# A two-layer MLP after sliding-window attention: its second product by Strassen's seven products

## The chip, the core and the metric

The kernel runs on one core of one Trainium2 chip. The engines are called as in the profile: PE is TensorE (matrix products), PEld its weight loads, DVE is VectorE, ACT is ScalarE, POOL is GpSimd, SP is SyncE, which here only issues DMAs. SBUF is the on-chip working memory, with 128 partitions; PSUM is the accumulator memory that PE writes to, in banks of 512 fp32 per partition. A semaphore is what one engine waits on for another. The metric is the device time of one launch in microseconds (us), as the median of several runs. Lower is better.

## The reference

Attention with a window of 128 and a bias that falls with distance, then layer norm, a two-layer MLP with ReLU, and the residual. Nothing else is computed.

```
# q, k, v: [8 batches, 8 heads, 576 positions, 64], fp32
scores = q k^T / 8 - slope[h] * |i - j|;  kept where 0 <= i - j < 128
attn   = softmax(scores);  x = (attn v), heads side by side   # x: [8, 576, 512]
mu  = mean(x);  var = mean((x - mu)**2)                       # over the 512 columns
xn  = (x - mu) / sqrt(var + 1e-06) * g_ln                     # g_ln: [512]
out = x + max(xn @ w_ch1, 0) @ w_ch2                          # w_ch1 [512, 2048], w_ch2 [2048, 512]
```

## The kernel before, in words

**Tiling.** The 8 x 576 rows are 36 blocks of 128 rows. `attention(i)` (line 571) takes one block from loads to the transposed and centred rows that the MLP reads. `mlp(c)` (line 932) takes one chunk of blocks; `CHUNKS` (line 267) has chunks of 3, 3, 2 and then seven of 4 blocks. "From the fourth chunk on" means these last seven, 28 blocks.

**The order.** Every piece of work is a `Task` with an engine, an assumed duration, the tasks that it needs, and a due value `v`. `Plan.run` (line 118) plays the whole kernel through as a list schedule: whenever an engine is free, it gives it the task that is ready and has the lowest `v`. The instructions are then emitted in that order, so each engine's queue is fixed before the launch. For a PE task that needs another engine's result, `SLACK` (line 294) makes the planner assume that the result comes 1.0 us later than it thinks. Attention is given a `v` that is 1.6 chunks ahead of the MLP (`av`, line 365; `LEAD`, `SPAN`). `PICK`, `PRI` and `HOLD` are tables of hand-set engine choices and shifts of `v`; their entries for MLP tasks are for the first three chunks.

**Attention of a block.** Scores on PE into `sc` (line 750), exponentials on ACT (line 798), a mask product on DVE (line 805), the product with v on PE into a bank of `fb` (line 822), then on DVE the reciprocal of the softmax sum (line 839) and the normalised rows `xb` (line 843, which also sums them through an accumulator that is read out as an instruction of its own). DVE then forms the mean (line 876), `xs` = (x - mean) * g (line 883, with g spread over the partitions in `g_t`, fp32), and the statistics (lines 864 and 870). A transposing DMA on SP's queue puts `xs` into `xt` (line 912). `rstd` = exp(-0.5 ln(var + eps)) is made on ACT, once for a chunk (lines 923 and 926). It isn't needed by the first product: since ReLU commutes with a positive factor of each row, it is applied at the very end.

**The MLP of a chunk.** First product: 16 groups A of four matmuls, each over up to 512 rows of the chunk (line 944), with 128 x 128 of `w1sb` as the stationary operand; ReLU on ACT or DVE puts each group into `ht` (lines 954 and 956). Second product: for each block 16 matmuls (B, line 972) with 128 x 128 of `ht` as the stationary operand and 512 columns of `w2sb` streamed; then one DVE instruction makes rstd * product + x (line 980) and one DMA on SP's queue stores the block (line 988). The last block is cut at column 384, so that most of its result is away before the last matmuls are done.

**Memory.** PE's work for the MLP, the transposes and the product with v share four PSUM banks, `fb`. `ht` has two buffers, `xt` three, `xb` sixteen blocks, `ot` (the results) four blocks. `qs`, `ks`, `qs16` and `ks16` are only used for the loads of blocks 0 to 5. POOL issues most loads of q, k, v and of the weights; SP the transposing DMAs and the stores. `keep_warm` (line 1009) fills PE with dummy products in the first 24 us.

Of the kernel before, what the change touches and what calls it, by code (L numbers as in the profile page):

```python
# [241 lines left out]
def kernel(  # L242
# [54 lines left out]
    HOLD = {'Za0': 3.13, 'k10.i': 55.05, 'cT0.11': 9.73, 'mreg20': 36.97, 'k8.i': 46.36, 'dist2a': 4.68}  # L297
    HEADS = 3
# [44 lines left out]
    xb = ring("xb", 16, [P, d_model], FP16)  # L343
# [3 lines left out]
    ot = ring("ot", 4, [P, d_model], FP32)  # L347
    st = ring("st", 4, [P, nc.vector.BN_STATS_DIM], FP32)
    mv = ring("mv", 4, [P, CB, nc.vector.BN_AGGR_DIM], FP32)
    lv = ring("lv", 2, [P, CB], FP32)  # L350
# [4 lines left out]
    g_row, one_t = ot[3][0:1, :], ot[2][0:1, 0:P]  # L355
# [93 lines left out]
    d_g = add("Gc", {"ACT": 0.6, "DVE": 0.69}, e_gc, [t_g], av(0, 4.5), rel="G")  # L449

# [120 lines left out]
    def attention(i):  # L571
# [240 lines left out]
        nm = []  # L812
        for half in range(2):
# [27 lines left out]
            def e_nm(e, b, half=half, key=key):  # L841
                pp = fb[plan.held[key][1]][:, 0 : 4 * (D + 1)].rearrange("p (h d) -> p h d", d=D + 1)
                nc.vector.scalar_tensor_tensor(  # L843
                    out=xb[i][:, 256 * half : 256 * half + 256].rearrange("p (h d) -> p h d", d=D),
# [5 lines left out]
                    accum_out=sums[i][:, half : half + 1],  # L850
# [4 lines left out]
            sums.writes(i, n_)  # L855
            rec.reads(2 * i + half, n_)
            xb.writes(i, n_)
            nm.append(n_)

        c = CHUNK_OF[i]  # L860
        j = i - FIRST[c]

        def e_bn(e, b):
            nc.vector.bn_stats(out=st[i][:, :], in_=xb[i][:, :])  # L864
        stats_v = max(av(i, 6.5), FIRST[c] / CB * SPAN - STATS_LEAD)
# [9 lines left out]
        def e_mu(e, b):  # L875
            nc.vector.tensor_scalar(
                out=mean[i][:, :], in0=sums[i][:, 0:1], scalar1=sums[i][:, 1:2], scalar2=1.0 / d_model, op0=ALU.add, op1=ALU.mult,
            )
        mu = add(f"mu{i}", ("DVE", 0.21), e_mu, nm, av(i, 6.5))
        sums.reads(i, mu); mean.writes(i, mu)  # L880

        def e_xs(e, b):
            nc.vector.scalar_tensor_tensor(  # L883
                out=xs[i][:, :], in0=xb[i][:, :], scalar=mean[i][:, 0:1], in1=g_t[:, :],
                op0=ALU.subtract, op1=ALU.mult,
            )
        xs_ = add(f"xs{i}", ("DVE", 0.75), e_xs, [mu, d_g], av(i, 6.6))
        mean.reads(i, xs_)
        xs.writes(i, xs_)
        xs_done[i] = xs_  # L890
        bn.deps.append(xs_)

        if i < X_BY_DMA:
# [15 lines left out]
            xt.writes(c, xt_)  # L909
        else:  # L910
            def e_xd(e, b):
                nc.sync.dma_start_transpose(out=xt[c][:, :, j * P : j * P + P], in_=xs[i][:, :])
            xi, xt_ = plan.transfer(f"XT{i}", "SP", 1.2, 0.85, 0.5, e_xd, [xs_], av(i, 7.0))
            xs.reads(i, xt_)
            xt.writes(c, xi)
        xt_done[i] = xt_

        if j == CHUNKS[c] - 1:
# [12 lines left out]

    def mlp(c):
# [4 lines left out]
        relu = []  # L937
        for f in range(NFB):
            key = f"A{c}.{f}"
            vm = v0 + f * per  # L940
# [7 lines left out]
            a = add(key, ("PE", 0.216 * nb), e_a, done + [t_w[f // 4][1]], vm, acq=("fb", key))  # L948
            xt.reads(c, a)

# [8 lines left out]
            relu.append(r_)  # L959
        for j in range(nb):  # L960
            i = FIRST[c] + j
            cuts = (0, 3 * P, d_model) if i == NBLK - 1 else (0, d_model)
            for c0, c1 in zip(cuts, cuts[1:]):
                key = f"B{i}" if c1 - c0 == d_model else f"B{i}.c{c0}"
                last = None
                for f0 in range(0, NFB, 4):
# [9 lines left out]
                    last = add(f"{key}.{f0}", ("PE", 0.864 * (c1 - c0) / d_model), e_b, relu[f0 : f0 + 4] + [t_w[4 + f0 // 4][1], last], vm, acq=("fb", key))  # L976
                    ht.reads(c, last)

                def e_o(e, b, i=i, j=j, key=key, c0=c0, c1=c1):
                    nc.vector.scalar_tensor_tensor(  # L980
                        out=ot[i][:, c0:c1], in0=fb[plan.held[key][1]][:, 0 : c1 - c0], scalar=rstd[c][:, j : j + 1],
                        in1=xb[i][:, c0:c1], op0=ALU.mult, op1=ALU.add,
                    )
# [20 lines left out]
    for c in range(len(CHUNKS)):  # L1004
        mlp(c)
# [46 lines left out]
```

## Time and profile before

| what | value |
| --- | --- |
| median of three runs (lowest, highest) | 320.42 us (320.11, 321.05) |
| span of the profiled execution | 317.5 us |
| mean granted TensorE clock over the span | 1.000 |
| PE busy | 311.3 us (98%) |
| DVE busy | 189.5 us (60%) |
| ACT busy | 161.0 us (51%) |
| POOL busy | 100.6 us (32%) |
| first product on PE (line 944) | 134.5 us busy, 640 matmuls |
| second product on PE (line 972) | 134.6 us busy, 592 matmuls |

The span runs from the first to the last instruction of one execution; the time of a run also holds what lies around it, 2.9 us between this span and the median. A matmul is pipelined, so the duration of one in the trace is longer than the distance from it to the next; how fast PE goes is read from the starts of long streaks. "Busy" counts overlapping matmuls once.

### The profile page before, as it was taken

The numbers are of one execution on the slowest core, as the hardware profiler recorded it, in microseconds if no ns is written. First come the engines' busy times: TensorE is split into PE (matmuls) and PEld (weight loads), VectorE is DVE, ScalarE is ACT, GpSimd is POOL, SyncE is SP. The second block draws the span as 40 slices with busy tenths as digits, with TensorE's granted clock in tenths as the row PEclk, the third lists the DMA queues.
The fourth block names the chain that finished last, engine by engine and source line by source line (L and its number), as shares of the span: only waits on it lengthen the run. The fifth ranks groups of instructions, "written<-read, shape, count | busy, mean of one in ns | idle before, by whom it ended". The sixth has DMA issues, their size and how long they took to land.

```text
span 317.5 us, 6575 instructions
## 1 busy us (share of the span) xinstructions
PE 311.3 (98%) x2580; PEld 178.3 (56%) x2580; DVE 189.5 (60%) x523; ACT 161.0 (51%) x258; POOL 100.6 (32%) x133
## 2 busy tenths in 40 slices
PE   8999999999999999999999999999999999999995
PEld 7777656765955544555555555545555455445543
DVE  3496788889866646764676467648654676221012
ACT  3657816872836732674267426742574257305600
POOL 5663469765633355434263234000000000000000
PEclk9999999999999999999999999999999999999999
DMA  8999999999999999999999999834600240011011
GB/s 176 248 219 205 196 140 167 168 148 117 162 178 158 174 138 173 171 166 131 171 189 154 100 135 172 108 52 116 118 17 19 83 85 18 21 66 66 2 66 66
DMA packets 156049, 40.15 MB, mean 126 GB/s; under 512 B 142577, under 2 KB 151025, under 8 KB 156018
## 3 DMA queue, kind: packets, MB, share of 16 engines
q0 software_dynamic: 101680, 16.65, 75.7%
q1 hardware_dynamic: 54336, 23.08, 40.9%
q8 instruction: 20, 0.33, 0.5%
q14 instruction: 11, 0.09, 0.1%
q10 hardware_dynamic: 2, 0.00, 0.0%
HBM read 36.70 MB, written 9.44 MB: 145 GB/s over the span
## 4 chain that ended last, share of the span: by engine, by line
PE 91%; DMA 5%; DVE 1%; SPq 0%; POOL 0%; issue 0%
PE fb L944 40%; PE fb L972 39%; PE sc L750 6%; PE fb L822 5%; DMA vxp<-in_v_dram 3%; DMA qs<-in_q_dram 2%; PE fb L714 1%; PE fb L1011 0%; SPq L483 0%; PE fb L897 0%; PE sc L766 0%; PE fb L666 0%; POOL qs L648 0%; POOL w1sb L562 0%; DVE mmix L469 0%
## 5 line engine op out<-in xcount | busy, mean ns | idle before, releaser
L972 PE MATMUL fb<-w2sb,ht 128*128 128x512 f16 (+2 forms) x592 | 134.6, 373 | 0.1
L944 PE MATMUL fb<-xt,w1sb 128*128 128x512 f16 (+2 forms) x640 | 134.5, 359 | 0.0
L956 ACT ACTIVATE ht<-fb 128x512 f16<-128x512 f32 (+2 forms) x142 | 79.5, 560 | 52.4 <-PE fb L944 50.7
L798 ACT ACTIVATE probs<-sc 128x1024 f16<-128x1024 f32 (+1 forms) x72 | 67.8, 973 | 69.2 <-PE sc L750 69.0
L944 PEld LDWEIGHTS <-w1sb 128*128 128x128 f16 x640 | 68.9, 114 | 47.1
L972 PEld LDWEIGHTS <-ht 128*128 128x128 f16 x592 | 54.0, 98 | 57.4 <-issue 0.3
L980 DVE SCALAR_TENSOR_TENSOR ot<-fb,rstd,xb 128x512 f32<-128x512 f32 (+2 forms) x37 | 27.2, 736 | 42.1 <-PE fb L972 41.8
L499 POOL DMA_DIRECT2D vx<-in_v_dram x36 | 30.4, 849 | 38.0 <-PE fb L822 21.1
L499 POOL DMA_DIRECT2D qk<-in_q_dram x34 | 28.5, 839 | 42.7 <-DMA qkt<-qk 22.6
L805 DVE TENSOR_TENSOR probs<-probs,mreg 128x1024 f16<-128x1024 f16 (+1 forms) x46 | 30.3, 676 | 13.9 <-ACT probs L798 13.7
L839 DVE RECIPROCAL rec<-fb 128x4 f32<-128x4 f32 x72 | 12.7, 179 | 36.7 <-PE fb L822 36.4
L822 PEld LDWEIGHTS <-probs 128*128 128x128 f16 x544 | 24.9, 97 | 13.1 <-issue 0.6
L843 DVE SCALAR_TENSOR_TENSOR xb<-fb,rec 128x256 f16<-128x256 f32 x72 | 30.3, 422 | 1.9
L499 POOL DMA_DIRECT2D qk<-in_k_dram x34 | 28.7, 847 | 7.0 <-DMA qk<-in_k_dram 2.1
L883 DVE SCALAR_TENSOR_TENSOR xs<-xb,mean,g_t 128x512 f16<-128x512 f16 x36 | 26.9, 748 | 0.7
L822 PE MATMUL fb<-vx,probs 128*128 128x65 f16 x496 | 27.2, 193 | 0.1
L864 DVE BATCH_NORM_STATS2 st<-xb 128x6 f32<-128x512 f16 x36 | 24.6, 683 | 0.0
L750 PEld LDWEIGHTS <-qkt 64*128 64x128 f16 x496 | 14.9, 94 | 11.9 <-issue 10.1
L750 PE MATMUL sc<-qkt 64*128 64x128 f16 x264 | 18.0, 216 | 0.0
L750 PE MATMUL sc<-qkt,qkt 64*128 64x128 f16 x208 | 14.7, 219 | 0.0
L954 DVE TENSOR_SCALAR ht<-fb 128x384 f16<-128x384 f32 (+2 forms) x18 | 10.4, 579 | 6.3 <-PE fb L944 6.0
L1011 PE MATMUL fb<-warm_t 128*128 128x128 f16 x122 | 10.6, 251 | 1.1 <-DVE warm_t L400 1.1
(71 smaller groups left out, 128.6 us busy)
## 6 DMA issues: line engine op xcount, KB each, us to landing
out_dram<-ot SPq DMA_DIRECT2D x35, 256.0 KB, 4.0
vx<-in_v_dram POOLq DMA_DIRECT2D x28, 128.0 KB, 9.8
qk<-in_q_dram POOLq DMA_DIRECT2D x26, 128.0 KB, 9.2
qk<-in_k_dram POOLq DMA_DIRECT2D x26, 128.0 KB, 10.1
w1sb<-in_moe_w_ch_dram POOLq DMA_DIRECT2D x4, 512.0 KB, 11.1
w2sb<-in_moe_w_ch_dram POOLq DMA_DIRECT2D x4, 512.0 KB, 14.2
ks<-in_k_dram SPq DMA_DIRECT2D x4, 256.0 KB, 6.5
qs<-in_q_dram SPq DMA_DIRECT2D x4, 256.0 KB, 6.2
```

The costliest lines, as they stand in the source:

```text
L499: nc.gpsimd.dma_start(out=dst(p0, n), in_=src[b, :, s0 : s0 + n, :].rearrange("h p d -> p h d"))
L750: nc.tensor.matmul(scs[half][:, g, c0 : c0 + P], kt[rows, 1, hp, :], qkt[i][rows, 0, hp, :], start=not bias, stop=True, skip_group_check=True,
L798: nc.scalar.activation(out=o, in_=n_, func=AF.Exp, scale=inv_sqrt_d)
L805: en.tensor_tensor(out=pv, in0=pv, in1=mask[:, 2 * half : 2 * half + 2, :, lo:], op=ALU.mult)
L822: nc.tensor.matmul(pp[:, hh * (D + 1) : hh * (D + 1) + D + 1], probs[i][:, bank, slot, side * P : side * P + P], vx[i if side else before] ...
L843: nc.vector.scalar_tensor_tensor(out=xb[i][:, 256 * half : 256 * half + 256].rearrange("p (h d) -> p h d", d=D), in0=pp[:, :, 0:D], scalar ...
L864: nc.vector.bn_stats(out=st[i][:, :], in_=xb[i][:, :])
L883: nc.vector.scalar_tensor_tensor(out=xs[i][:, :], in0=xb[i][:, :], scalar=mean[i][:, 0:1], in1=g_t[:, :], op0=ALU.subtract, op1=ALU.mult,)
L944: nc.tensor.matmul(fb[b][:, 0:n_], w1f[f // CB][:, kb, f % CB, :], xt[c][:, kb, 0:n_], start=(kb == 0), stop=(kb == NKB - 1),)
L956: nc.scalar.activation(out=ht[c][:, f, 0:n_], in_=src, func=AF.Relu)
L972: nc.tensor.matmul(pm[:, 0 : c1 - c0], ht[c][:, f, j * P : j * P + P], w2sb[f // CB][:, f % CB, c0:c1], start=(f == 0), stop=(f == NFB - 1),)
L980: nc.vector.scalar_tensor_tensor(out=ot[i][:, c0:c1], in0=fb[plan.held[key][1]][:, 0 : c1 - c0], scalar=rstd[c][:, j : j + 1], in1=xb[i][: ...
```

## The change

The second product of a chunk is, with H the 512 x 2048 rows after ReLU and W the 2048 x 512 matrix `w_ch2`, cut in two halves each way. Instead of eight products of halves it computes seven, of sums and differences of the halves (the form of Strassen's method with fewest additions, due to Winograd). Each of the seven is 16 matmuls that stream 256 columns; before, a chunk's second product was 64 matmuls that stream 512.

- `weight_sums` forms four sums of the quarters of `w_ch2` once, eight DVE subtractions, in the memory of `qs` and `ks`.
- In each of the seven chunks DVE forms four sums of quarters of `ht`, in two instructions each (`sa`, `sb` into the memory of `qs16` and `ks16`; `sc`, `sd` in place in `ht`).
- The products alternate between two PSUM banks, X and Y. DVE adds what lies in a bank to the result (`ra` to `rg`, seven instructions of 512 elements; before, four). A product that accumulates onto the one before it in its bank, or starts the bank anew, waits for the read of that bank.
- The residual and the products can only be added if no factor of a row comes after. So in these chunks the rows are normalised ahead of the first product: `xs` = (x - mean) * rstd, with mean and rstd per partition, and g is multiplied into the rows of `w_ch1` on chip (`scale_weights`, 16 DVE instructions, after the third chunk's first product has read `w_ch1`). rstd is now formed for two blocks at a time and stands ahead of `xs`; the two blocks' transposing DMAs come after it. The mean of line 876 and the accumulator of line 843 fall away in these chunks.
- `gcol` is g with its 512 values down the partitions, from four small matmuls.
- The groups A of these chunks run in the order 0, 8, 1, 9, ..., so that the halves' sums can start early.
- `xb` is kept and released by chunk and `ot` by two blocks (three buffers of two); the cut of the very last block at column 384 is gone; in the last chunk each block is stored in two halves of its columns.

```diff
+    SEVEN = 3
+    SUMS_V = 40.0
...
-    xb = ring("xb", 16, [P, d_model], FP16)
+    xb = ring("xb", 4, [P, CB, d_model], FP16)
-    ot = ring("ot", 4, [P, d_model], FP32)
+    ot = ring("ot", 3, [P, 2, d_model], FP32)
+    gcol = sb("gcol", [P, NKB], FP32)
...
+    def e_gk(e, b):
+        for kb in range(NKB):
+            nc.tensor.matmul(fb[b][:, kb : kb + 1], g_row[:, kb * P : kb * P + P], one_t[:, 0:1], start=True, stop=True)
...
+    t_gk = add("Gk", ("PE", 0.5), e_gk, [t_g], av(2, 4.0), acq=("fb", "Gk"))
+    d_gk = add("Gkc", ("DVE", 0.2), e_gkc, [t_gk], av(2, 4.5), rel="Gk")
...
+        fast = c >= SEVEN
...
-                    accum_out=sums[i][:, half : half + 1],
+                    accum_out=None if fast else sums[i][:, half : half + 1],
...
+        elif j % 2 == 0:
+            todo = []
+        else:
+            def e_ln(e, b):
+                nc.scalar.activation(out=lv[i][:, 0:2], in_=mv[c][:, j - 1 : j + 1, 1], func=AF.Ln, bias=eps_t[:, :])
+            def e_rs(e, b):
+                nc.scalar.activation(out=rstd[c][:, j - 1 : j + 1], in_=lv[i][:, 0:2], func=AF.Exp, scale=-0.5)
...
+            for x, y in ((i - 1, j - 1), (i, j)):
+                def e_xs(e, b, x=x, y=y):
+                    nc.vector.tensor_scalar(
+                        out=xs[x][:, :], in0=xb[c][:, y, :], scalar1=mv[c][:, y, 0:1], scalar2=rstd[c][:, y : y + 1],
+                        op0=ALU.subtract, op1=ALU.mult,
+                    )
+                xs_ = add(f"xs{x}", ("DVE", 0.3), e_xs, [rs], av(x, 6.6))
...
+    def weight_sums():
...
+            for n, (dst, a, b_) in enumerate(((o[0], b12, b11), (o[2], b22, b12), (o[1], b22, o[0]), (o[3], b21, o[1]))):
+                def emit(e, b, dst=dst, a=a, b_=b_):
+                    nc.vector.tensor_tensor(out=dst, in0=a, in1=b_, op=ALU.subtract)
+                t = add(f"sumT{h}.{n}", ("DVE", 0.69), emit, got[h][-1:] + [t_w[4 + h][1], t_w[6 + h][1]], SUMS_V)
...
+    def scale_weights():
+        for m in range(CB):
+            def emit(e, b, m=m):
+                for kb in range(NKB):
+                    nc.vector.tensor_scalar(out=w1sb[m][:, kb, :], in0=w1sb[m][:, kb, :], scalar1=gcol[:, kb : kb + 1], scalar2=None, op0=ALU.mult)
+            scaled.append(add(f"scaleW{m}", ("DVE", 0.9), emit, plain[m] + [d_gk, t_w[m][1]], FIRST[SEVEN] / CB * SPAN - 8.0))
+
+    def seven(c, relu, v0):
+        A, B_ = slice(0, FOURTH), slice(FOURTH, 2 * FOURTH)
...
+        def product(n, k, key, lhs, rhs, first, deps):
+            for p in range(2):
+                for h in range(2):
+                    def emit(e, b, p=p, h=h):
+                        o = fb[plan.held[key][1]][:, FOURTH * p : FOURTH * p + FOURTH]
+                        for f in range(CB * h, CB * h + CB):
+                            nc.tensor.matmul(o, lhs(f, p), rhs(f), start=first and f == p == 0, stop=f == F2 - 1, skip_group_check=True)
+                    t = add(f"{k}{c}.{p}{h}", ("PE", 0.436), emit, deps[h] + [last.get((key, p))], v0 + (4 * n + 2 * p + h) * step, acq=("fb", key))
...
+        def read(name, key, out, in1, deps, n, rel=None):
+            def emit(e, b):
+                src = fb[plan.held[key][1]][:, :].rearrange("p (n c) -> p n c", n=2)
+                nc.vector.tensor_tensor(out=out, in0=src, in1=in1, op=ALU.add)
+            return add(f"{name}{c}", ("DVE", 0.75), emit, deps, v0 + (4 * n + 4) * step - 12.0, rel=rel)
...
+            s1.append(sums("sa", h, ssum[0][h], h_[:, lo(h), B_], h_[:, hi(h), B_], ALU.add, low + high, v))
+            s2.append(sums("sb", h, ssum[1][h], ssum[0][h], h_[:, lo(h), A], ALU.subtract, [s1[h]], v))
...
+        p1 = list(product(0, "Pa", x_, at(0, 0), w_lo, True, [low[h] + w[0:2] for h in range(2)]))
+        r1 = read("ra", x_, oa[:, :, A], xa[:, :, A], p1, 0)
+        p2 = list(product(1, "Pb", y_, at(F2, 0), w_hi(0), True, [high[h] + w[2:4] for h in range(2)]))
+        r2 = read("rb", y_, oa[:, :, A], oa[:, :, A], p2 + [r1], 1)
+        for h in range(2):
+            s3.append(sums("sc", h, h_[:, lo(h), B_], h_[:, lo(h), A], h_[:, lo(h), B_], ALU.subtract, [s1[h]], v0 + h))
+            s4.append(sums("sd", h, h_[:, hi(h), A], h_[:, hi(h), A], ssum[1][h], ALU.subtract, [s2[h]] + [t for t in p2 if t.name[-1] == str(h)], v0 + 4 + h))
+        p3 = list(product(2, "Pc", x_, ss(1), ts(1), False, [[s2[h], r1, sumT[h]] for h in range(2)]))
+        r3 = read("rc", x_, oa[:, :, B_], xa[:, :, B_], p3, 2)
+        p4 = list(product(3, "Pd", y_, ss(0), ts(0), True, [[s1[h], r2, sumT[h]] for h in range(2)]))
+        r4 = read("rd", y_, ob[:, :, B_], xb_[:, :, B_], p4, 3)
+        p5 = list(product(4, "Pe", x_, at(0, 2), ts(2), False, [[s3[h], r3, sumT[h]] for h in range(2)]))
+        r5 = read("re", x_, ob[:, :, B_], ob[:, :, B_], p5 + [r4], 4)
+        p6 = list(product(5, "Pf", y_, at(F2, 0), w_hi(1), False, [[s4[h], r4] for h in range(2)]))
+        r6 = read("rf", y_, oa[:, :, B_], oa[:, :, B_], p6 + [r3], 5, rel=y_)
+        p7 = list(product(6, "Pg", x_, at(F2, 2), ts(3), False, [[r5, sumT[h]] for h in range(2)]))
+        r7 = read("rg", x_, ob[:, :, A], xb_[:, :, A], p7, 6, rel=x_)
...
     def mlp(c):
...
+        order = [x for n in range(NFB // 2) for x in (n, n + NFB // 2)] if fast else range(NFB)
...
-            a = add(key, ("PE", 0.216 * nb), e_a, done + [t_w[f // 4][1]], vm, acq=("fb", key))
+            a = add(key, ("PE", 0.216 * nb), e_a, done + [scaled[f // CB] if fast else t_w[f // CB][1]], vm, acq=("fb", key))
...
+        if fast:
+            seven(c, [relu[f] for f in range(NFB)], v0 + 16 * per)
+            return
...
-            cuts = (0, 3 * P, d_model) if i == NBLK - 1 else (0, d_model)
+            cuts = (0, d_model)
```

## The prediction: working and numbers

> **What bounds the kernel now.** I read the page's busy shares, its forty slices and its chain first.
>
> ```profile
> PE 311.3 (98%) x2580; PEld 178.3 (56%) x2580; DVE 189.5 (60%) x523; ACT 161.0 (51%) x258; POOL 100.6 (32%) x133
> ...
> PE   8999999999999999999999999999999999999995
> ...
> DVE  3496788889866646764676467648654676221012
> ...
> PEclk9999999999999999999999999999999999999999
> ...
> PE 91%; DMA 5%; DVE 1%; SPq 0%; POOL 0%; issue 0%
> ```
>
> A busy PE need not be a full PE, but here the chain (the work that ended last, followed back) is 91% PE, and its DMA part is the first loads. PE sets the time, at full clock in every slice. DVE is at most at nine tenths, and that before the seven chunks begin. Next, the chain in order of time (start, us, engine and line): its last pieces, then the loads and attention's pace.
>
> ```profile
> 231.30 0.55 PE sc L750 x16
> ...
> 263.56 0.55 PE sc L750 x16
> ...
> 272.50 13.81 PE fb L972 x64
> 286.31 13.81 PE fb L944 x64
> 300.13 13.87 PE fb L972 x80
> 314.02 0.35 DVE ot L980
> ```
>
> A chunk's second product costs 13.81 us (215.8 ns a matmul), with no gap to the first product of the next. Four blocks later the same scores come 263.56 - 231.30 = 32.26 us on: 27.62 us of the two products and 4.6 us of attention. That is the period in which DVE must do its share too. Then the timeline of PE for matmuls of 256 columns, which the third chunk (two blocks) has in its first product (start, us, matmuls):
>
> ```profile
> 83.82 2.79 PE L944 MATMUL fb<-xt,w1sb 128*128 128x256 f16 x24
> ```
>
> It is followed back in the chain as 2.62 us for 24, so 109.2 ns each, though every one has a weight load of its own. Last, the groups by shape (busy us, mean ns of one), for DVE's prices.
>
> ```profile
> L805 DVE TENSOR_TENSOR probs<-probs,mreg 128x1024 f16<-128x1024 f16 x44 | 29.4, 687 | 13.0 <-ACT probs L798 12.9
> ...
> L883 DVE SCALAR_TENSOR_TENSOR xs<-xb,mean,g_t 128x512 f16<-128x512 f16 x36 | 26.9, 748 | 0.7
> L980 DVE SCALAR_TENSOR_TENSOR ot<-fb,rstd,xb 128x512 f32<-128x512 f32 x35 | 26.3, 750 | 41.9 <-PE fb L972 41.5
> ...
> L876 DVE TENSOR_SCALAR mean<-sums 128x1 f32<-128x1 f32 x36 | 7.7, 213 | 1.0
> ...
> L843 DVE DVE_READ_ACCUMULATOR xb<-fb,rec 128x1 f32 x72 | 6.0, 83 | 0.0
> ...
> L454 DVE TENSOR_SCALAR sid<-iden 128x128 f16<-128x128 f16 x8 | 1.7, 358 | 0.0
> ...
> L469 DVE COPY mmix<-mreg 128x2048 f16<-128x2048 f16 x1 | 0.7, 683 | 0.0
> ```
>
> **PE, the gain.** Per chunk 7 x 16 = 112 matmuls at 109.2 ns are 12.23 us in place of 13.81: 1.58 us less. Seven chunks give 11.1 us; the last chunk counts 0.06 more, since its cut block goes. All of it is on the path, as PE never pauses there. The split of the sum costs 1.7 ns a matmul (109.2 against 215.8 / 2); without it the eighth saved would be 12.1 us.
>
> A rule of the Trainium skill speaks against this: "TensorE: Matmul & The Clock Gate", section "Part 3: Packing small matmuls", says a weight load overlaps a running matmul only if it goes to other rows of the array, and section "LDWEIGHTS" prices a load of 128 columns at some 107 ns. By that estimate a load would be paid for every matmul, 48 more per chunk, 5.1 us against the gain, and the kernel would be some 25 us slower. The 109.2 ns row leaves no room for such a load; the trace decides, and the sum goes by it.
>
> **DVE, what it must carry.** Per chunk it loses four evictions (4 x 750 ns), four means (4 x 213) and eight accumulator reads (8 x 83): 4.5 us. `xs` becomes a single-source fp16 operation, which no row shows at 512 elements; 128 elements take 358 ns by mean (1.7 us busy for 8, so 213 each) and a copy of 2048 takes 683. Between the two, (683 - 213) x 384 / 1920 above 213 is 307 ns; four save 4 x 441 = 1.8 us. It gains seven reads of a bank (at 750, the eviction they resemble) and eight half sums (at 687, the mask product with as many elements): 10.8 us. Net 4.5 us a chunk. In the six windows from 200 to 260 us DVE is busy 37.1 us, 20.0 per period; 24.5 of a new period of 30.7 is 80%. It doesn't become the bound; whether it answers in time is the question.
>
> A product waits for the read two products back, in its bank. Beside it runs the other bank's product, 1.75 us. The read is answered 0.22 us after PE (the idle before the last eviction), takes 0.75 and needs about 0.1 to come back: 1.07. So 0.68 us are left for a queue, about one other DVE instruction. Behind a late read stand the bank, the next product and, in DVE's order, the mask products and row sums of attention. Cover: the planner counts 1.0 us more for what PE waits for and then takes a group A of the next chunk (0.86 us) or attention in between; two banks stay free for it. Without cover, one further DVE instruction ahead of every read would be up to 0.69 us x 49 products. Bounds for the seven chunks: 0 to 34 us. I take 1.4 us, 0.2 a chunk, nearer the low end, because of the 80%. The last chunk has no next one, but no attention either; its 7 reads, 4 late `sa`/`sb` halves and `sc`/`sd` come to some 9 us in 12.2.
>
> **The seam at the fourth chunk.** Two blocks of DVE work come once. Eight weight sums at 687 ns, 5.5 us, due at 40, can be done from about 45 us on; windows 50 to 80 us show DVE busy 8.65, 9.15 and 9.34 of 10, and blocks from the ninth on give back about 0.8 us each (0.44 + 0.21 + 0.17) there. Scaling `w_ch1` is 16 instructions at 307 ns, 4.9 us (213 to 683: 3.4 to 10.9), and stands between the third chunk's first product (ends 88.15) and the fourth's (begins 95.34). DVE idles some 4 us from 86 to 98. Behind the scaling on DVE's queue lie mask products and evictions; PE has the third chunk's second product, 6.9 us, and two blocks' attention to do meanwhile. Cover gone, it would be all of both, 10.4 us. I take 1.0, bounds 0 to 10.
>
> **Rows and DMAs.** `xs` waits for statistics (0.68 + 0.18), two ACT steps (0.29 + 0.21) and for its neighbour; the transposing DMAs leave SP in pairs, one block (8 us) later for the first. The cover is the lead: block 11's `xs` starts at 79.03, lands 6.4 later, and is needed at 95.34. What lies behind on ACT (exponentials, ReLU) and on SP (transposes, stores) shifts by 1 to 2 us within that lead; price without cover, some 2 us once. POOL's loads are not moved; they stop at about 200 us, eight blocks ahead of the scores. ACT gains 0.5 us a chunk at 51%: nothing. The four matmuls for `gcol` (nearest row: fp32, 640 ns, two pieces) fall among warming products: 0, at most 2.6. Releasing `xb` by chunk and `ot` by pairs: 0, covered by three spare chunks and stores that land in 4.0 us.
>
> **The end.** Before, the last matmul is followed by 0.22, an eviction of 0.35 from 314.02, and 3.1 us until the span's end. Now it is a read of 0.75 (+0.4), then two stores, of which the second is issued about 0.5 later (SP's issues take 0.5 to 0.57 in the chain), each 128 KB between the landings of 1.7 (64 KB) and 2.0 (192 KB): +0.15. Together 1.05, bounds 0.4 to 2.
>
> **Sum.** -11.1 + 1.4 + 1.0 + 1.05 = -7.65. The span would be 309.85 and the median of runs, which lies 2.9 above the span, 312.8 us. A measurement of this kernel tells about 0.3% (1 us) from no change.
>
> **Rivals.**
> - The seam fails (0.13): the sums and the scaling hold up the fourth chunk by half of their 10.4 us, 5 us more than zero, 4 more than assumed: 316.8; all of it, 322. For it: DVE above nine tenths just before. Against: the second product of the third chunk, and idle DVE after 86 us.
> - Reads answer late (0.18), slower: DVE's fixed order puts mask products and half sums ahead of the reads, and PE stands at each product. It decides from (11.1 - 2.05) / 49 = 0.18 us of waiting for each product. With one instruction more than the slack, half of the time, 0.34 us each, it is 16.9 us: 328.3. For it: 80% and a queue in order. Against: PE's spare work from the next chunk.
> - The saved matmuls cost more than the row says (0.05), also slower: if 256 columns went at the mean that attention's 65 columns have for their duration (193 ns, an unpipelined figure), 112 x 0.193 = 21.6 us, 7.8 more a chunk: 375. The 109.2 ns speak flatly against it, and the stationary operands are now `ht` pieces, whose loads are the shorter (98 against 114 ns).
>
> **How the numbers follow.** My forecast, 0.64, gives 312.8 and by itself 309.5 to 316: all waits zero and the short end at the one side, 3 us more of waits at the other. Most of the first rival lies below 319.5, part of the second just above. The range 309.2 to 320.2 leaves out about 0.18, nearly all above. Faster by over 0.3%: 0.64 + 0.11 of the first rival = 0.75. Within: 0.02 of each of the first two, 0.04. Slower: the rest, 0.21.
>
> **What would show it.** The products' line should have 112 matmuls a chunk at 109 ns and the period between scores should be near 30.7. The chain should stay PE; DVE in it near 95 us is the seam, DVE at the reads' line is the second rival. DVE should be busy 189.5 + 31.5 + 10.4 = 231 us. The prediction is wrong if the streaks of products in the last chunk show pauses, if PE idles more than 5 us after 90 us, or if `xs` at 512 elements takes far more than 0.3 us.

## The result, and the profile after

The changed kernel takes 312.19 us in the median of four runs, beside 320.53 for the kernel before. One of the four, 316.76 us at a mean granted clock of 0.986, fell in a slower state and is left out of the ratio; the median of the other three is 312.07 us. The ratio is 0.9741, with a 95% interval from 0.9713 to 0.9769. The profiled execution spans 309.3 us, 8.2 less than the 317.5 before, and itself ran in 311.27 us.

The page of the changed kernel gives the busy shares, three rows of its forty slices and the chain that ended last by engine. Line 1104 is now the first product, line 1022 the seven products, line 1137 the old second product of the first three chunks, and line 1030 DVE's read of a bank.

```profile
span 309.3 us, 7229 instructions
...
PE 301.1 (97%) x2902; PEld 210.2 (68%) x2902; DVE 223.9 (72%) x541; ACT 162.4 (53%) x271; POOL 100.8 (33%) x133
...
PE   7999999999999999999999999999999999999993
...
DVE  3497699989986589956985898569858985840372
...
PE 95%; DMA 1%; DVE 1%; SPq 0%; ACT 0%; POOL 0%; issue 0%; DVEq 0%
```

PE still sets the time, with 10 us less of work. DVE went from 60% to 72%, and its row now swings: eights and nines, then fives and sixes, once in every four slices or so. That swing is the period of a chunk, and the experiments come back to it. The chain in order of time, at the same places as before:

```profile
143.26 0.55 PE sc L768 x16
...
173.94 0.55 PE sc L768 x16
...
280.31 12.09 PE fb L1104 x56
292.39 12.25 PE fb L1022 x112
304.64 0.02 issue
304.67 0.69 DVE ot L1030
```

112 matmuls take 12.25 us where 64 (80 in the last chunk, with its cut) took 13.81 to 13.87, and the same scores come 30.68 us apart where it was 32.26. The span can be cut at three points, and the parts add up:

| stretch | before | after | difference |
| --- | --- | --- | --- |
| to the first matmul of the first product | 24.37 | 25.35 | +0.98 |
| from there to the fourth chunk's second product | 88.00 | 88.79 | +0.79 |
| from there to the last matmul's end | 201.63 | 190.50 | -11.13 |
| from there to the end of the span | 3.50 | 4.66 | +1.16 |
| sum | 317.50 | 309.30 | -8.20 |

(The fourth chunk's second product begins at 112.37 before and 114.14 after; its last one ends at 314.00 and 304.64.) In the third row the loss is nothing: seven chunks at 1.58 us and the cut of the last block make the forecast 11.1. Of the first row, 0.69 us is a wait that the trace shows: the first product's first matmul waits for `xt`, which ACT copies out of PSUM once PE has transposed the rows. Before, other matmuls stand between those transposes and the first product, and there is no wait (first before, then after; start, duration, and in brackets the idle time ahead of it):

```profile
24.37 2.11 PE L944 MATMUL fb<-xt,w1sb 128*128 128x384 f16 x12
```

```profile
25.35 1.46 PE L1104 MATMUL fb<-xt,w1sb 128*128 128x384 f16 x8 [0.69 <-ACT xt L950]
```

The durations that the prediction had to estimate are in the groups by shape (busy us, mean ns of one, idle before):

```profile
L1030 DVE TENSOR_TENSOR ot<-fb,xb 128x512 f32<-128x512 f32 x28 | 19.3, 690 | 8.3 <-PE fb L1022 8.0
...
L1030 DVE TENSOR_TENSOR ot<-fb,ot 128x512 f32<-128x512 f32 x21 | 14.4, 687 | 7.4 <-PE fb L1022 7.4
...
L927 DVE TENSOR_SCALAR xs<-xb,mv,rstd 128x512 f16<-128x512 f16 x28 | 10.5, 418 | 2.6 <-ACT rstd L920 2.6
...
L1012 DVE TENSOR_TENSOR qs<-ht 128x1024 f16<-128x1024 f16 x14 | 9.7, 692 | 13.7 <-ACT ht L1118 13.5
...
L999 DVE TENSOR_SCALAR w1sb<-w1sb,gcol 128x512 f16<-128x512 f16 x16 | 5.4, 396 | 0.0
```

A read takes 690 ns (750 assumed), a half sum 692 (687), `xs` 418 (307) and a piece of the scaling 396 (307).

### The profile page after: what moved, and what is told of

It is laid out like the page before. It is cut to its first block, busy times and chain, and to the rows that moved or that the text cites. A ratio compares the mean times of both kernels' runs of the same rounds, so it can differ in the third digit from the quotient of the medians.

```text
span 309.3 us, 7229 instructions
## 1 busy us (share of the span) xinstructions
PE 301.1 (97%) x2902; PEld 210.2 (68%) x2902; DVE 223.9 (72%) x541; ACT 162.4 (53%) x271; POOL 100.8 (33%) x133
## 3 DMA queue, kind: packets, MB, share of 16 engines
q0 software_dynamic: 101680, 16.65, 78.0%
## 4 chain that ended last, share of the span: by engine, by line
PE 95%; DMA 1%; DVE 1%; SPq 0%; ACT 0%; POOL 0%; issue 0%; DVEq 0%
PE fb L1104 41%; PE fb L1022 28%; PE fb L1137 9%; PE sc L768 6%; PE fb L843 6%; DMA qs<-in_q_dram 1%; PE fb L1179 1%; PE fb L684 1%; PE fb L732 1%; PE sc L784 1%; PE fb L940 0%; SPq L501 0%; PE fb L447 0%; PE fb L461 0%; POOL qs L666 0%; DVE ot L1030 0%
## 5 line engine op out<-in xcount | busy, mean ns | idle before, releaser
L1104 PE MATMUL fb<-xt,w1sb 128*128 128x512 f16 (+2 forms) x640 | 136.3, 359 | 1.0 <-ACT xt L950 0.7
L816 ACT ACTIVATE probs<-sc 128x1024 f16<-128x1024 f32 (+1 forms) x72 | 67.6, 972 | 28.4 <-PE sc L768 28.3
L1022 PEld LDWEIGHTS <-ht 128*128 128x128 f16 x560 | 52.9, 98 | 10.0
L1022 PE MATMUL fb<-w2sb,ht 128*128 128x256 f16 x336 | 42.3, 273 | 0.0
L1137 PE MATMUL fb<-w2sb,ht 128*128 128x512 f16 x128 | 31.6, 380 | 0.3 <-DVE xb L864 0.3
L517 POOL DMA_DIRECT2D qk<-in_k_dram x34 | 29.4, 868 | 2.1 <-DMA w1sb<-in_moe_w_ch_dram 1.8
L1022 PE MATMUL fb<-ks,ht 128*128 128x256 f16 x224 | 28.0, 273 | 0.0
L1030 DVE TENSOR_TENSOR ot<-fb,xb 128x512 f32<-128x512 f32 x28 | 19.3, 690 | 8.3 <-PE fb L1022 8.0
L1030 DVE TENSOR_TENSOR ot<-fb,ot 128x512 f32<-128x512 f32 x21 | 14.4, 687 | 7.4 <-PE fb L1022 7.4
L1012 DVE TENSOR_TENSOR qs<-ht 128x1024 f16<-128x1024 f16 x14 | 9.7, 692 | 13.7 <-ACT ht L1118 13.5
L1137 PEld LDWEIGHTS <-ht 128*128 128x128 f16 x128 | 11.5, 97 | 11.2 <-issue 0.6
```

Of the source, the lines that this page charges most:

```text
L517: nc.gpsimd.dma_start(out=dst(p0, n), in_=src[b, :, s0 : s0 + n, :].rearrange("h p d -> p h d"))
L816: nc.scalar.activation(out=o, in_=n_, func=AF.Exp, scale=inv_sqrt_d)
L1022: nc.tensor.matmul(o, lhs(f, p), rhs(f), start=first and f == p == 0, stop=f == F2 - 1, skip_group_check=True)
L1030: nc.vector.tensor_tensor(out=out, in0=src, in1=in1, op=ALU.add)
L1104: nc.tensor.matmul(fb[b][:, 0:n_], w1f[f // CB][:, kb, f % CB, :], xt[c][:, kb, 0:n_], start=(kb == 0), stop=(kb == NKB - 1),)
L1137: nc.tensor.matmul(pm[:, 0 : c1 - c0], ht[c][:, f, j * P : j * P + P], w2sb[f // CB][:, f % CB, c0:c1], start=(f == 0), stop=(f == NFB - 1),)
```

## The experiments

Twelve kernels. Three ask where the loss outside the products lies and whether it can be had back; two take the change apart; five load DVE to find how far the reads were from mattering; the first is the changed kernel itself, as the thing to compare with, and the last puts together what helped. Each was timed beside the kernel before, and ratios are to that kernel, with 95% intervals.

### The changed kernel again

> The changed kernel as it is, on the chip of the next three, to compare them with. Every theory expects the 312.2 us measured before, within 0.5 us, a span near 309 to 310.5 us and a mean granted clock near 0.993.

312.05 us, ratio 0.9742 (0.9712 to 0.9771), span 309.5. As expected in time, but the profile shows a full clock from 10 to 16 us, where the first profile of the same kernel had shown half speed:

```profile
11.00:12.00 1.00, 1.00 (x15) 0.95 (x13) 0.44 (x2) 0.77 (x3) 0.00 (x0) 0.83 1.28 292
12.00:13.00 1.00, 1.00 (x17) 0.65 (x15) 0.00 (x0) 0.69 (x2) 0.80 (x2) 0.50 1.24 232
13.00:14.00 1.00, 1.00 (x10) 0.96 (x8) 0.53 (x2) 0.89 (x2) 1.00 (x2) 0.50 1.23 228
14.00:15.00 1.00, 1.00 (x14) 0.98 (x12) 0.82 (x5) 0.00 (x0) 1.00 (x2) 0.50 1.14 204
```

(Windows of the first profile of the changed kernel: length, then the busy time and count of PE, PEld, DVE, ACT and POOL, the granted clock, DMA's share and GB/s.) The clock column falls to 0.50 there. In the second profile the first matmul of the first product starts at 25.21 us all the same, against 25.35. So the first product doesn't start later for the slow stretch, 3.4 us at half clock among dummy products and first attention work. That doesn't make the stretch free. In the 25 runs of the kernel before that were timed beside the fifth to the eighth kernel here, the 19 with a mean clock of 0.998 or more have a median of 319.80 us, the 6 at 0.992 to 0.994 one of 321.10 (a stretch of 3.4 us at half clock lowers the mean of a 318 us span by 0.5 x 3.4 / 318 = 0.005). Runs with it are some 1.3 us longer; where in the kernel that time goes isn't shown. Differences of 1 us between two kernels below have to be read with this in mind.

### gcol's matmuls later

```diff
     t_g.deps.append(first_turn[0])
+    t_gk.deps.append(pv_done[3])
```

> The four small fp32 matmuls for gcol are moved from 9.8 us to after the fourth block's product with v, near 30 us. Theory: they and their wait are thin work on PE just before the granted clock falls to half from 11.8 to 15 us, and the fall is theirs; without them the clock stays at 1.00 there, the first MLP matmul starts near 24.4 us as before the change in place of 25.35, and the kernel takes about 311.2 us (1.0 us less). Rival: the clock falls because the loads land at other times than before, whatever gcol does; then the clock still shows half speed near 12 us and the time stays at 312.2, or gains only the 1.0 us that the matmuls themselves occupy if they stood on the path.

311.06 us, ratio 0.9717 (0.9685 to 0.9748), span 309.3. The median is 1.0 us lower, as the theory had it, but its reason falls. The clock was full here, but it was full in the run above too, which has the matmuls early, and it falls in the profile of the kernel before cut to 256 columns (0.70 from 11 to 12 us, then 0.50), which has no such matmuls at all. And the first product starts at 25.79, not at 24.4. Over the profiles of all these kernels it starts between 24.37 and 26.96 us; two profiles of the same kernel differ there by 0.14 us, and kernels that are alike up to there by more than 1. One thing does follow the edit: the wait of 0.69 us for `xt` ahead of the first product stands in all ten profiles with gcol's matmuls early, and in none of the other four (here the matmuls for gcol stand in its place). The intervals overlap with those of the changed kernel, and only one of the six runs above had a mean clock of 0.998 or more, against four of the six here. A gain is likely; how much of the 1.0 us is the wait and how much the clock isn't shown.

### The weight sums later

```diff
+                t.deps.append(pv_done[13])   # for each of the eight weight sums
```

> The eight weight sums wait for the product with v of the fourteenth block (near 91 us) in place of starting at 44 us. Theory: between 40 and 56 us DVE is full (9.9 of 10 from 40 to 50) and the sums make the pauses of PE at 41.5 and 53.4 us, some 0.5 us each; later they lie in DVE's free time: 0.5 to 1.0 us less, 311.2 to 311.7, and DVE below 9 of 10 from 40 to 50 us. Rival (the seam): DVE is now too full from 83 to 100 us, where the scaling of the first weights is, and the fourth chunk starts later: 1 to 4 us more, 313 to 316.

311.77 us, ratio 0.9749 (0.9707 to 0.9790): no difference that can be told. In the trace both theories are half right. The pause of 0.5 us near 53.5 us is gone, the one near 42.5 stays (0.37), and DVE is busy 6.8 us of 10 from 40 to 50 us in place of 9.9. In exchange PE pauses 0.3 us at 98.7, where DVE now has the scaling and the sums. The pause near 42.5 isn't the sums' doing alone: it stands in the kernel without any sums too (PE idle for 0.22 us in the experiment on the rows alone, 0.30 in the changed kernel), and it is missing from several profiles that have the sums early.

### The last read cut by blocks

```diff
+                    nc.vector.tensor_tensor(out=ob[:, p, A], in0=fb[...][:, FOURTH * p : FOURTH * p + FOURTH], in1=xb_[:, p, A], op=ALU.add)   # p = 0, 1
```

> In the last chunk the last read of a bank is cut in two, one for each block, so that the first of the two last stores leaves while PE still does the second block. Theory of the end: 0.3 us less of DVE after the last matmul and 0.5 us less for the second store, 0.8 us together: 311.4. Rival: the end is set by one store's landing and the end of the program, whatever goes before it: 0.3 us at most, 311.9.

311.96 us, ratio 0.9742 (0.9708 to 0.9776). From the last matmul's end to the end of the span it is 4.42 us, 0.24 less. The edit didn't do what was meant: both halves of the read started after the last matmul, at 305.61 and 305.95, though the first half's matmuls were over at 304.70. It fits that both halves lie in one PSUM bank that PE was still filling (until 305.57). So the theory of the end wasn't tried here; it is in the last experiment.

### The rows alone

```diff
-        if fast:
-            seven(c, [relu[f] for f in range(NFB)], v0 + 16 * per)
-            return
...
+                    if fast:
+                        nc.vector.tensor_tensor(out=ot[...], in0=fb[...], in1=xb[c][:, j, c0:c1], op=ALU.add)
```

> One part of the change alone: rows normalised ahead, g put into W1, the pairs' rstd, xb by chunk and ot by pairs; but the second product is the 64 matmuls of 512 columns as before, with an eviction that only adds, and there are no sums and no weight sums. Theory: the whole gain is in the matmuls saved, so this lands within 1 us of before, 319.5 to 321.5, with the period between chunks at 32.25 us as before. Rival one: the lighter DVE work of the rows (about 3.3 us a chunk less) is worth something by itself; then below 319. Rival two: the scaling of W1 holds up the fourth chunk; then 322 to 325 and PE idle between 80 and 100 us.

(The edit also puts the groups A back in plain order and the cut of the last block back at column 384.)

321.41 us, ratio 1.0057 (1.0025 to 1.0088): slower than before by about 1.8 us, at the edge of what the theory allowed. Its first product starts late (26.60), and from there to the last chunk's second product it takes 276.12 us against 275.76 before: 0.36 us for the normalised rows and the scaling, and no pause between 80 and 110 us. So the rows bring nothing by themselves, although DVE is less busy (182.4 us against 189.5); they are what the products cost as an entry fee.

### The kernel before, by 256 columns

```diff
+                            for a in range(c0, c1, 256) if c >= 3 else (c0,):
+                                z = min(a + 256, c1) if c >= 3 else c1
-                                pm[:, 0 : c1 - c0], ht[...], w2sb[f // CB][:, f % CB, c0:c1],
+                                    pm[:, a - c0 : z - c0], ht[...], w2sb[f // CB][:, f % CB, a:z],
```

> The kernel before with each matmul of the second product from the fourth chunk on cut in two of 256 columns, each with its weight load: 448 matmuls and loads more, no product saved. Theory (109.2 ns for 256 columns against 215.8 for 512): 128 x 109.2 - 64 x 215.8 = 0.17 us a chunk, 1.2 us in all, 321.5. Rival, by the Trainium skill, page TensorE: Matmul & The Clock Gate, sections Part 3 and LDWEIGHTS (a load of 128 columns, some 107 ns, isn't hidden under a matmul on the same rows): 448 x 0.107 = 48 us more, 368.

321.36 us, ratio 1.0064 (1.0036 to 1.0092), so 1.5 us more. The chain's last pieces and the weight loads' group of this kernel:

```profile
288.37 13.81 PE fb L944 x64
302.18 14.03 PE fb L974 x144
```

```profile
L974 PEld LDWEIGHTS <-ht 128*128 128x128 f16 x1040 | 97.2, 98 | 23.4 <-issue 0.3
```

The last chunk's second product takes 14.03 us in place of 13.87, 0.16 more (0.17 expected). 448 weight loads more are in the trace, 98 ns each, and beyond those 0.16 us a chunk nothing of them is seen in the time. The rule of the Trainium skill that a load overlaps a running matmul only if it goes to other rows of the array ("TensorE: Matmul & The Clock Gate", section "Part 3: Packing small matmuls") doesn't hold for these streaks; by an estimate from it the kernel would have taken some 368 us. The same section excepts a load into the background weight buffer; whether that is what happens here no run shows.

### One more DVE instruction ahead of each read

```diff
+                for _ in range(1):   # 2 in the next experiment
+                    nc.vector.tensor_tensor(out=spare[:, :, :], in0=tsum[0][:, 0:CB, :], in1=tsum[1][:, 0:CB, :], op=ALU.add)
                 src = fb[plan.held[key][1]][:, :].rearrange("p (n c) -> p n c", n=2)
```

> The changed kernel with one more DVE instruction (a sum of 128x1024 fp16 into spare memory, 0.6 us from start to start, 0.69 alone) just ahead of each of the 49 reads of a bank, unknown to the planner. Theory: the changed kernel's last chunk shows a read done 0.86 us before the bank is wanted again, so one instruction fits there and costs nothing but 0.6 us at the very end; in the full chunks DVE goes from some 24.5 to 28.7 us of a period of 30.7, 94%, and costs 0 to 5 us in all: 312.5 to 317.5. Rival: reads are on the path already, and 0.6 x 49 = 29 us come: 341.

320.93 us, ratio 1.0029 (1.0006 to 1.0051): the whole gain is gone. Both expectations miss it. The span is 318.3 us, 8.9 more than the changed kernel's 309.3 to 309.5, and the scores come 177.21 - 145.09 = 32.12 us apart. Of these 8.9 us the five chunks with attention beside them (the fourth to the eighth, called full here) lose 1.4 to 1.8 each, and the last two 0.7 each. The chain of the last chunk shows how PE waits there:

```profile
303.41 0.60 DVE spare L1031
304.01 0.61 DVE ot L1033
304.62 0.04 issue
304.66 9.02 PE fb L1023 x80
```

The third product waits for the first read. In the changed kernel that read is in time, but only just (timeline of its last chunk, DVE and PE):

```profile
294.40 0.68 DVE L1012 TENSOR_TENSOR ht<-ht 128x1024 f16<-128x1024 f16 x1
295.00 0.68 DVE L1030 TENSOR_TENSOR ot<-fb,xb 128x512 f32<-128x512 f32 x1
295.60 0.68 DVE L1012 TENSOR_TENSOR ht<-ht,ks 128x1024 f16<-128x1024 f16 x1
...
295.73 1.03 PE L1022 MATMUL fb<-qs,ks 128*128 128x256 f16 x8
```

The read stands behind three half sums, ends at 295.68, and the product that waits for it begins at 295.73. The 0.86 us of room that the expectation went by belongs to the later reads of this chunk. The first read is this tight only in the last two chunks. In the full chunks attention and groups A stand between the products, and every read ends 1.3 to 2.2 us before the product that waits for it begins. There PE loses its time in more places. Matmul by matmul against the changed kernel, whose order is the same, a full chunk's 1.4 us are 0.50 at products that wait for a read, 0.23 at attention's matmuls that wait for a mask product, and 0.70 at groups A of the next first product that wait for a bank to be emptied, by DVE's row normalisation or by a late read (line 1107 is the first product here; two of its waits in the sixth chunk, in brackets):

```profile
197.36 1.02 PE L1107 MATMUL fb<-xt,w1sb 128*128 128x512 f16 x4 [0.17 <-DVE xb L865]
198.56 2.75 PE L1107 MATMUL fb<-xt,w1sb 128*128 128x512 f16 x12 [0.18 <-DVE ot L1033]
```

### Two of them

> The same with two instructions ahead of each read. Theory: 1.2 us is more than the 0.86 us to spare, so the last chunk's products wait about 0.35 us each (5 or 6 times, 2 us), and in the six other chunks DVE has 24.5 + 8.4 = 32.9 us for a period of 30.7: DVE becomes the bound there and each takes 2.2 us more, 13 us; with 1.2 at the end 328 us or somewhat more, DVE above 95% busy from 114 us on. Rival: what is spare in the next chunk's first product covers this too, and it stays below 318.

353.18 us, ratio 1.1023 (1.0982 to 1.1063), and the scores come 37.20 us apart. Far above the 328 of the theory: that counted DVE's work against the period, 32.9 us, and PE's period grew to 37.2 with DVE idle for a part of it. By the list of waits (us, times, longest) PE waits 21.5 us at the products for the reads' line, where the list of the changed kernel has no such wait, and 7.3 us at groups of the first product:

```profile
PE fb L1023 <- DVE ot L1033: 21.5, 25, 1.2
...
PE fb L1107 <- DVE ot L1033: 4.1, 5, 0.9
...
PE fb L1107 <- DVE xb L865: 3.2, 4, 0.8
```

### Ahead of the first two reads, and ahead of the last five

> One more DVE instruction of 0.6 us, unknown to the planner, ahead of the first two reads of each chunk only (14 in all); ahead of all 49 it cost 8.8 us. Theory: DVE's queue is thick where a chunk's products begin, where the half sums and the mask products of attention stand with the first reads (in the changed kernel's last chunk the first read ends 0.05 us before its bank is wanted), and has room afterwards: this costs most of it, 5 to 8 us, 317 to 320. Rival: the price is spread evenly, as DVE's share over the period would have it: 14/49 of 8.8, 2.5 us, 314.6.

312.84 us, ratio 0.9792 (0.9756 to 0.9828): less than either expectation had.

> The same ahead of the third to the seventh read of each chunk only (35 in all). Theory of the thick beginning: 0.6 us at the very end and little else, 312.6 to 315. Rival, even price: 35/49 of 8.8, 6.3 us, 318.4.

314.16 us, ratio 0.9822 (0.9785 to 0.9860). That lies in the range of the thick beginning, but the run before it has refuted the theory itself: the first two reads don't carry the price. Nor is the price even. From the fourth chunk's second product to the span's end, which leaves out where the first product happened to start, these two cost 1.3 and 1.6 us (by the ratios 1.6 and 2.6, each to about 1.2 us), and all 49 at once 9.0. The 1.3 us of the first two reads lie in the last two chunks alone, where the first read was tight.

The seventh chunk, a full one, shows where DVE's room is. It is cut into the stretch of its products (with the attention and the groups that stand between them) and what follows up to the next chunk's products; each cell has the length and, behind the stroke, how long DVE is busy in it, in us.

| DVE work added in a chunk's products, 0.6 us each | products | the rest | period | lost |
| --- | --- | --- | --- | --- |
| none | 16.65 / 15.11 | 14.02 / 8.72 | 30.67 | |
| 2 (1.2 us) | 16.65 / 16.03 | 14.02 / 8.71 | 30.67 | 0.0 |
| 5 (3.0 us) | 16.65 / 16.34 | 14.27 / 9.90 | 30.91 | 0.2 |
| 7 (4.2 us) | 17.43 / 17.12 | 14.69 / 10.34 | 32.12 | 1.4 |
| 14 (8.4 us) | 21.06 / 20.55 | 16.13 / 11.44 | 37.20 | 6.5 |

What a chunk takes in without loss is some 2.8 us (3.0 - 0.2, 4.2 - 1.4; at 14 it is 1.9). The forecast's average had promised 30.7 - 24.5 = 6.2 us. In the products' stretch of the changed kernel DVE is busy 91%, and 1.5 us are free. What is more than that DVE does late, in the first product that follows: with five instructions PE loses nothing at the products and 0.24 us at one group of that first product, which waits for the last read. The windows of the changed kernel show the two stretches for the fourth chunk: DVE is the third pair of numbers.

```profile
110.00:120.00 10.00, 10.00 (x115) 7.22 (x113) 8.81 (x19) 6.45 (x10) 4.95 (x6) 1.00 2.00 156
120.00:130.00 10.00, 10.00 (x121) 8.40 (x121) 9.15 (x20) 4.47 (x5) 6.46 (x8) 1.00 1.80 152
130.00:140.00 10.00, 10.00 (x76) 5.70 (x75) 5.83 (x15) 6.28 (x12) 3.54 (x5) 1.00 1.86 173
```

From 114 to 130 us PE does a chunk's products and DVE is busy nine tenths; from 130 on it does the next first product and DVE is free four tenths. Of the room in the second stretch only a little is of use to work that is due in the first: some 1.3 us, the 2.8 less the 1.5. This account was formed from these runs; the next one bears on it.

### The planner told of it

```diff
-            return add(f"{name}{c}", ("DVE", 0.75), emit, ...)
+            return add(f"{name}{c}", ("DVE", 1.35), emit, ...)
```

> The instruction ahead of all 49 reads again, but the planner is told of it (a read is planned at 1.35 us in place of 0.75), so it can put first-product groups of the next chunk and attention between the products. Theory of the cover: what was lost for want of planning comes back, as DVE has 28.7 us of work for a period of 30.7: 313 to 316 in place of 320.9. Rival: DVE can't do more in the stretch of the products whatever the order; then it stays near 320.

314.96 us, ratio 0.9860 (0.9807 to 0.9914), span 311.8, with the same 49 instructions that cost 8.9 us untold. The scores come 179.91 - 149.24 = 30.67 us apart: the first four full chunks lose nothing, though each has 4.2 us more of DVE work. So the room of the first product can be used, but only by an order that was made for it. The seventh chunk shows what the planner did: 17.10 / 16.13 us in the products' stretch and 13.58 / 10.84 in the rest, in the table's terms. It did not set more groups of the first product between the products (two, as before); it moved DVE's work for attention, in this chunk one of six mask products, one of five row normalisations and both `xs`, out of that stretch. What is lost, 2.0 us from the fourth chunk's second product on, is 0.6 at the first read of each of the last two chunks, which have no attention to move, a pause of 0.4 at 255.6 us that waits for a ReLU, and small things.

### gcol later and the end in two banks

```diff
+    t_gk.deps.append(pv_done[3])
...
+                        apart = final and key == x_
+                        o = fb[plan.held[key + str(p)][1]][:, 0:FOURTH] if apart else fb[plan.held[key][1]][:, FOURTH * p : FOURTH * p + FOURTH]
```

> A version meant to beat both: gcol's matmuls later (311.06 alone), and in the last chunk the X products of the two halves of the rows in two PSUM banks, so that the first half's reads don't wait for the second half's matmuls, each block's last store follows its own read, and the last read is of 256 columns. Theory: 1.0 us for the first as measured, and for the end 0.3 us of DVE and 0.4 of a store issued behind another: 310.3 to 310.7. Rival: the end is set by the last store's landing alone; then 311.0 as with the first edit only.

310.74 us, ratio 0.9718 (0.9696 to 0.9741), the lowest median of all. After the last matmul (304.97) there are some 4.05 us to the span's end at 309.0, against some 4.67: 0.6 of the 0.7 us expected. The last two reads begin at 304.57 and 305.01, one after the other. By the medians it is 1.3 us below the changed kernel, by the ratios 0.7 to 0.8; the two intervals overlap by three thousandths (0.9712 to 0.9741), so against the kernel before it is clear, against the changed kernel only likely. Later matmuls for gcol alone had a ratio of 0.9717, so what the two banks bring is seen at the end of the trace and not in the times of the runs.

## Why the prediction was right, and where it was lucky

**The gain.** 11.1 us were forecast and 11.13 measured, from the one row of 256-column matmuls in the trace before (109.2 ns). The kernel before cut into 256 columns confirms the row and refutes the rival that the weight loads would show. This part was worked out and not luck.

**Rows and DMAs.** Forecast: nothing. The rows alone cost 0.36 us after the first product's start. The four matmuls for gcol were to fall among warming products at no cost; with them early the first product waits 0.69 us for `xt`, and the median is perhaps 1 us higher, within the bound of 2.6 that was given.

**The end.** 1.05 us forecast, 1.16 measured; two banks, which shorten the last read and let each store follow its own, take 0.6 of it back. That fits the reading of it (a longer read, a second store behind the first).

**The seam.** 1.0 us was put on the fourth chunk's start. PE doesn't pause there at all: it is busy 10 us of 10 from 80 to 110 us. A loss of about the same size (0.8 us) lies before it, mostly in pauses near 42.5 and 53.5 us; with the sums moved away the second is gone, and a shorter one comes at 98.7. The step "Two blocks of DVE work come once" named the work and put its price in the wrong place. That the size agrees is luck: the first pause comes without the sums too.

**The reads.** 1.4 us forecast, none measured. Here the number was near and the reasoning not. The step that failed is "So 0.68 us are left for a queue, about one other DVE instruction". It counted only the other bank's product beside a read and put groups A and attention down as cover. In the full chunks these do stand there, and a read has 1.3 to 2.2 us to spare; in the last chunk the later reads have 0.86 and the first 0.05. And the cover named for it, that the planner puts other work between the products, holds in full only for what the planner knows: 49 instructions unknown to it cost 8.9 us, known to it they cost four of the five full chunks nothing. The rival of late reads was set to decide from 0.18 us of waiting per product; 0.6 us more of DVE work ahead of each read reached that as an average, though only a third of a full chunk's loss was at products that wait for a read, and the time was that of the kernel before. DVE's 80% over the period (76% as measured from 200 to 260 us) was the wrong figure to judge by; 91% in the stretch of the products is the right one.

**The sum** was -7.65 and -8.20 was measured. The first two rows of the table lose 0.98 + 0.79 us, 0.77 more than the 1.0 put on the seam; the reads cost 1.4 less, the end 0.1 more. The errors cancel to half a microsecond.

DVE's busy time was forecast at 231 us and is 223.9. `xs` and the scaling are longer than assumed (3.1 and 1.4 us of sums of durations more), the reads shorter (3 us less). The rest is overlap: neighbouring instructions overlap a little (a read lasts from 295.00 to 295.68, the sum behind it starts at 295.60) and busy time counts that once. The durations of all DVE instructions add up to 28.4 us more than its busy time, and to 19.9 more before. For `xs` the prediction said that no row shows a single-source fp16 operation at 512 elements; the trace before has one, though from PSUM, that would have given the 418 ns almost exactly (busy us, mean ns of one):

```profile
L905 DVE COPY xt<-fb 128x512 f16<-128x512 f16 x4 | 1.7, 420 | 0.8 <-PE fb L897 0.7
```

The 0.307 us came from a straight line between 213 ns from start to start at 128 elements, where one lasts 358, and the duration of a copy at 2048. `xs` was a sign of being wrong if it took far more than 0.3 us; it took 0.11 more, without harm, as DVE had the room. The two other signs didn't come: PE never idles in the windows from 90 us on while there are products to do, and the last chunk's streak has no pause.

What stays open: why the first product starts anywhere from 24.4 to 27.0 us, and so how much of the table's first row, beyond the wait of 0.69 us, belongs to the change; and where the 1.3 us of the runs with a stretch at half clock go.

## What to carry to other kernels

When PE is the bound, a saving in matmuls can be priced from the start-to-start distance of the same shape in the trace, and here it arrived whole, as the work handed to another engine was in time. Judge that engine by the stretch in which PE waits for it, not by its share of a period: 76% on average was 91% in the stretch, and the room was 2.8 us and not 6. In a fixed order, room elsewhere counts for little (here some 1.3 us a chunk) unless the plan knows what it is to hold; tell the plan the true durations before trusting it to hide them.

## What the runs showed of the hardware

- The granted clock fell to half for 3.4 us, somewhere between 11.4 and 16.8 us, in five of the fourteen profiles, and not in every profile of one kernel (1.00 until after the last matmul in the second profile of the changed kernel). The first product's start didn't follow it (25.35 with the fall, 25.21 without), but of 25 runs of the kernel before, those with a lower mean clock were 1.3 us longer (321.10 against 319.80).
- A fp16 operation of one source on DVE over 512 elements took 418 ns (`xs`) and 396 (scaling) by mean, well above the 307 read off between 128 and 2048 elements and near the 420 of a copy of 512 out of PSUM; the 2048-element copy varied as well, 683 ns before and 1062 for one of the two after.
- Two DVE reads of one PSUM bank both began after the last matmul into that bank (305.61 and 305.95, matmuls until 305.57), though one read only the half that was finished at 304.70; in two banks the first began ahead of the last matmul's end (304.57 against 304.97). Whether the chip or the order of waits in the program makes the first case wait isn't shown.
